# A Fourier convolution with a mixture of experts: the order of loads, gathers, scatters and gates behind the last Fourier middle

## The chip, the cores and the metric

The kernel runs on one core of one Trainium2 chip. The metric is device time in microseconds (us), the median of the runs. Engines are named as the profile names them: PE is TensorE (PEld its weight loads), DVE VectorE, ACT ScalarE, POOL GpSimd, and SP SyncE, which here only issues transfers.

## The reference, cut to what matters

```python
X = np.fft.rfft(x, axis=1)                  # x: 8 x 3072 x 256
Y = X * (filt_r + 1j * filt_i)[None]
x = np.fft.irfft(Y, n=3072, axis=1).reshape(8 * 3072, 256)
logits = x @ w_gate                         # 8 experts
expert_idx = np.argmax(logits, axis=1)
# gate_w: softmax probability of the chosen expert
# an expert keeps its first 768 tokens, in order
h = np.maximum(np.einsum('ecd,edf->ecf', disp, w1), 0.0)   # 256 -> 1024
y = np.einsum('ecf,efd->ecd', h, w2)                       # 1024 -> 256
out[i] = gate_w[i] * y[expert_idx[i], pos[i]]              # 0 for tokens not kept
```

## The kernel before, in words

The first part convolves batch after batch by a discrete Fourier transform in two steps on PE. As the experts are full after some two batches, only batches 0 and 1 and the first rows of batch 2 are transformed. `Conv.middle` multiplies by the filter, goes back by one step and leaves the result in the tiles V; `ti` transposes V on DVE, and `ai` (for the last batch `ai_last`) makes the rows and the router's logits, which SP writes to the DRAM buffer ybuf (L406). `route` finds each token's place in its expert and builds, by matmuls with one-hot tiles (L517), the table of tokens by slot; `row_of_slot` (L134) makes of it the index idxg.

The second part takes the 8 experts in order. An expert has 6 tiles of 128 tokens, in two chunks of three, (e, 0) and (e, 1). POOL gathers a chunk's rows from ybuf by three indirect DMAs (`gather`, L537). `turn` transposes them (L551, 12 matmuls) and splits them into a high half xh on ACT (L558) and a low half xl on DVE (L562). `up_steps` has 8 steps of 6 matmuls of 384 columns (L577), each followed by a split of h on ACT and DVE. `down_steps` has one step for each tile, 24 matmuls (L629); ACT scales the result by the token's gate into ob (L632) and POOL scatters it to the output (L633). `gate` makes the softmax gate of a chunk in six small DVE operations and an Exp on ACT (L596); for the chunks (0, 0) and (1, 0) it is `early_gate`, which starts at L849.

`load_part` brings a weight: a plain load of the 1024 KB to the tile raw (L660), four or two cuts on ACT that leave the rounded half wah or wbh and the negative of it in wal or wbl, and then a DMA on POOL's queue that adds the weight to that from DRAM (L673, `accum_op=ALU.add`), 512 KB each. `zero` writes 2 MB of zeros to the output (L142); `zero_late` does so beside the loads of later experts.

What sets the order is the program text: under `tc.manual_schedule()` every engine runs its instructions as they are written, and each engine's queue is first in, first out. Chunk (0, 0) and chunk (1, 0) are gathered early, while the last batch is still being made. PSUM has seven banks in rotation. The stretch between the last middle and `steady`, as it stands before:

```python
R[e, 1] = load_rows(e, 1)        # for e = 0, 1
up((1, 0), (), 1)
prep((0, 1))                     # turn and gate
up((0, 1), (), 0)
load_a, cut_a = load_part(2, "a", raw, w0)
load_a()
R[2, 0] = load_rows(2, 0)
down((1, 0), idxs0)
prep((1, 1))
up((1, 1), list(cut_a), 1)
R[2, 1] = load_rows(2, 1)
down((0, 1))
```

Of the kernel before, what the change touches and what calls it, by code (L numbers as in the profile page):

```python
# [13 lines left out]
ALU = mybir.AluOpType  # L14
# [74 lines left out]
def fftconv_moe_kernel(ctx, tc, x, fr, fi, fny, wg, w1, w2, ca, cai, cb, co, out, cap):  # L89
    nc = tc.nc  # L90
# [4 lines left out]
    NTOK = NB * SEQ  # L95
    NB0 = min(NB, -(-E * cap // SEQ) + 1)
    NF = FF // 128
    NE = min(3, NT)
    EE = 2
# [22 lines left out]
    idxs = glob.tile([128, NSLOT], I32, name="idxs")  # L122
    idx0 = glob.tile([128, EE * NT], I32, name="idx0")
    idxs0 = glob.tile([128, EE * NT], I32, name="idxs0")
# [23 lines left out]
    def zero_late(n):  # L148

        for _ in range(min(n, len(zlate))):  # L150
            apart(zero(zlate.pop(0)), "scatter", "rows behind the tokens that are routed ahead of the branch")

    def apart(ins, group, reason):
        tc.declare_no_dep(ins.ins, group=group, reason=reason)
        tc.add_to_no_dep_group(group, ins.ins)
# [7 lines left out]
    def run(fs):  # L163
        for f in fs:
            f()
# [366 lines left out]
    W, X, Gt, H = {}, {}, {}, {}  # L532
# [31 lines left out]
    def new_H(ci, n=3):  # L564
        h = hps[ci].tile([128, 2, NF, chunks[0][1] * 128], F32R, name="h", tag="h")[:, :, :, :n * 128]
        return [h[:, 0], h[:, 1]]

    def up_steps(e, x, hs, t0, n):
        o = slice(t0 * 128, (t0 + n) * 128)

        def step(m):
            (xh, xl), (ah, al) = x, W[e][:2]
            ps = bank()
            k = 0
            for kk in range(2):
                for w, y in ((ah, xh), (ah, xl), (al, xh)):
                    nc.tensor.matmul(ps[:, :n * 128], w[:, kk, m * 128:(m + 1) * 128], y[:, kk, o], start=k == 0, stop=k == 5)  # L577
                    k += 1
            split(hs[0][:, m, :], hs[1][:, m, :], ps[:, :n * 128], True)
        return [lambda m=m: step(m) for m in range(NF)]  # L580

    R, sm = {}, {"group": "scatter"}
# [3 lines left out]
    def load_rows(e, ci):  # L586
        t0, n = chunks[ci]
        rows = sm["rows"].tile([128, n, CH], F32, name="rows", tag="rows", bufs=sm["nrows"])
        gather(rows, idxg, e * NT + t0, n, (NB0 - 1) * SEQ + LAST * N2)
        return rows  # L590
# [12 lines left out]
    def prep(k):  # L603
        rows, n = R.pop(k), chunks[k[1]][1]
        X[k] = turn(rows, n, sm["p"])
        lg = sm["p"].tile([128, n, E], F32, name="lg", tag="lg")
        nc.vector.tensor_tensor(out=lg, in0=rows[:, :, 128:136], in1=rows[:, :, 136:144], op=ALU.add)
        gate(lg, n, k)

    def up(k, fill=(), place=None):  # L610
        n = chunks[k[1]][1]
        H[k] = new_H(k[1] if place is None else place)
        for m, f in enumerate(up_steps(k[0], X.pop(k), H[k], 0, n)):
            f()
            if fill and m % 2:
                fill.pop(0)()

    def down_steps(k, ix=None):
        e, (t0, n) = k[0], chunks[k[1]]
        hh, hl = H.pop(k)  # L620
        bh, bl = W[e][2], W[e][3]
        gt = Gt.pop(k)

        def step(i):
            ps = bank()
            o = slice(i * 128, (i + 1) * 128)
            for m in range(NF):
                for j, (y, w) in enumerate(((hh, bh), (hh, bl), (hl, bh))):
                    nc.tensor.matmul(ps[:, :D], y[:, m, o], w[:, m, :], start=m == 0 and j == 0, stop=m == NF - 1 and j == 2)  # L629
            ob = sm["p"].tile([128, D], F32, name="ob", tag="ob", bufs=4)  # L630
            j = e * NT + t0 + i
            nc.scalar.activation(out=ob, in_=ps[:, :D], func=AF.Copy, scale=gt[:, i:i + 1])  # L632
            ins = nc.gpsimd.indirect_dma_start(out=out, out_offset=bass.IndirectOffsetOnAxis(ap=(idxs if ix is None else ix)[:, j:j + 1], axis=0),  # L633
                                               in_=ob, in_offset=None, bounds_check=NTOK - 1, oob_is_err=False)
            apart(ins, sm["group"], "the slots' tokens differ")
        return [lambda i=i: step(i) for i in range(n)]

    def down(k, ix=None):
# [8 lines left out]
        nc.vector.tensor_tensor(out=te, in0=te, in1=tf, op=ALU.add)  # L647
        nc.vector.tensor_copy(ix, te)

    def load_part(e, part, raw, pool, parts=2, dma=None, add=True):  # L650

        src = w1[e].rearrange("(k p) f -> p k f", p=128) if part == "a" else w2[e].rearrange("(k p) d -> p k d", p=128)
        shape = [128, src.shape[1], src.shape[2]]
        h, l = (pool.tile(shape, F32R, name="w" + part + c, tag="w" + part + c, bufs=1) for c in "hl")
        W.setdefault(e, [None] * 4)[slice(0, 2) if part == "a" else slice(2, 4)] = [h, l]
        box = []

        def load():
            box.append(raw.tile(shape, F32, name="raw", tag="raw"))
            (dma or nc.sync).dma_start(out=box[0], in_=src)  # L660

        def cut(k):
            w = shape[1] * shape[2] // parts
            r, fh, fl = (t.rearrange("p n f -> p (n f)")[:, k * w:(k + 1) * w] for t in (box[0], h, l))
            nc.scalar.copy(fh, r)
            if not add:
                nc.gpsimd.tensor_tensor(out=fl, in0=r, in1=fh.bitcast(F32), op=ALU.subtract)
                return
            nc.scalar.activation(out=fl, in_=r, func=AF.Copy, scale=-1.0)
            if (k + 1) * 2 % parts == 0:  # L670
                n = shape[1] // 2
                o = slice((k * 2 // parts) * n, (k * 2 // parts + 1) * n)
                nc.gpsimd.dma_start(out=l[:, o, :], in_=src[:, o, :], accum_op=ALU.add)  # L673
        return load, [lambda k=k: cut(k) for k in range(parts)]

    def load_w(e, raw, pool):
        cuts = []
        for part in "ab":
            load, cut = load_part(e, part, raw, pool)
            load()  # L680
            zero_late(1)
            cuts += cut
        return cuts

# [80 lines left out]
    with tc.manual_schedule():  # L765
# [44 lines left out]
        for b in range(NB0 - 1):  # L810
# [5 lines left out]
            counts, sums, slots, masks, table = route(L, False, (ohp, ohp))  # L816
# [7 lines left out]
            if b + 2 == NB0:  # L824
                side_ctx.close()
                w0 = run_ctx.enter_context(tc.tile_pool(name="w0", bufs=1, side="right"))
                raw0 = run_ctx.enter_context(tc.tile_pool(name="raw0", bufs=1, side="right"))
# [9 lines left out]
        b = NB0 - 1  # L837
# [9 lines left out]
        def early_gate(e):  # L847
            lg = ep.tile([128, NE, E], F32, name="lg", tag="lg", bufs=2)
            nc.vector.tensor_tensor(out=lg, in0=early_x[e][:, :, 128:136], in1=early_x[e][:, :, 136:144], op=ALU.add)  # L849
            gate(lg, NE, (e, 0))  # L850
# [4 lines left out]
        def early_row(e, t):  # L855
# [2 lines left out]
        fill[0].append(cut_a[0])  # L858
        fill[1] += [early_index, cut_a[1]]
        fill += [[cut_a[2], lambda: early_row(0, 0)], [cut_a[3], load_b, lambda: early_row(0, 1)], [lambda: early_row(0, 2)], [last_fill],  # L860
                 [cut_b[0]], [cut_b[1]], [cut_b[2]], [cut_b[3]]]
        cv.middle(V, fill, ahead, last=[early_turn])
        top_ctx.close()
        w1p = run_ctx.enter_context(tc.tile_pool(name="w1p", bufs=1, side="right"))
        hps = [run_ctx.enter_context(tc.tile_pool(name="hp0", bufs=1, side="right"))]
        ep1 = run_ctx.enter_context(tc.tile_pool(name="ep1", bufs=1, side="right"))
        es = top_ctx.enter_context(tc.tile_pool(name="es", bufs=1))
        load_a, cut_a = load_part(1, "a", raw0, w1p, 4, add=False)
        load_b, cut_b = load_part(1, "b", raw0, w1p, 4, nc.gpsimd)
        load_a()  # L870
        L = new_L(True)
        counts, sums, slots, masks, table = route(L, True, (ohp, ohp))
# [11 lines left out]
        ti(V, 3, 4)  # L884
        run([early[4], cut_a[0], early[5], cut_a[1], early[6], cut_a[2], early[7], cut_a[3]])
        load_b()
        early_gate(0)
        for q in range(2, 4):
            ti(V, q)
        run(first)  # L890
        sm["p"] = es
        later = down_steps((0, 0), ix=idxs0)
        later[0]()
        run(counts)
        run(rest[:1])
        sums()
        run(cut_b[:2])
        run(rest[1:])
        run(slots)
        run(cut_b[2:3])  # L900
        later[1]()
        run(cut_b[3:])
        run(masks)
        X[1, 0] = turn(early_x[1], NE, ep1)
# [11 lines left out]
        smp = run_ctx.enter_context(tc.tile_pool(name="sm", bufs=2))  # L916
        raw = run_ctx.enter_context(tc.tile_pool(name="raw", bufs=2))
        sm.update(p=smp, rows=smp, nrows=3)
        for e in range(EE):
            R[e, 1] = load_rows(e, 1)  # L920
        scatter_rows(idxs, NSLOT)
        up((1, 0), (), 1)
        prep((0, 1))
        up((0, 1), (), 0)
        load_a, cut_a = load_part(2, "a", raw, w0)
        load_a()
        R[2, 0] = load_rows(2, 0)
        down((1, 0), idxs0)
        prep((1, 1))
        up((1, 1), list(cut_a), 1)  # L930
        R[2, 1] = load_rows(2, 1)
        down((0, 1))
        load_b, cut_b = load_part(2, "b", raw, w0)
        load_b()
        for ci in range(NC):
            prep((2, ci))
        later = down_steps((1, 1))
# [107 lines left out]
```

## Time and profile before

| | |
|---|---|
| time, median of 3 runs | 506.05 us (505.30 to 507.09) |
| profiled execution: time, span | 507.01 us, 505.30 us |
| PE busy | 482.8 us (96%) |
| ACT, DVE, POOL busy | 268.6, 238.6, 198.8 us |
| mean granted PE clock | 0.984 of full speed |
| moved by DMA | 96.01 MB |

The span runs from the first to the last instruction; the time of the same execution is 1.71 us longer. Times in the text are us from the span's start. The Fourier part ends in the last middle (about 160 to 193 us). Behind it the rows of the last batch and the first chunks of experts 0 and 1 are mixed (193 to 222), then come the remaining chunks of these two experts (222 to 291), and from 291 us on `steady` for experts 2 to 7. In a row of the timeline or of the waits, "<-" in brackets names the instruction that ended an engine's idle time; it is put down to the one that came last by the profile.

### The profile page before, as it was taken

To read this page: it belongs to the slowest core of one execution; us is meant where nothing else is said; L and a number is where in the kernel's file an instruction comes from. 1 tells how busy PE (TensorE), PEld (TensorE's weight loads), DVE (VectorE), ACT (ScalarE), POOL (GpSimd) and SP (SyncE) were. 2 spreads that over 40 slices of the span, in tenths; PEclk is the share of its full clock that TensorE was granted. 3 is DMA by queue.
4 is the path that set the end of the run, shared out by engine and by line. 5 is a ranking of instruction groups with operands and counts; after the bars stand their busy time and mean duration, and the time that the engine had idled before them with its cause. 6 is when DMAs were issued, how large, how long until landed. Compare 5 with 4: busy or idle time off the path is not lost.

```text
span 505.3 us, 10342 instructions
## 1 busy us (share of the span) xinstructions
PE 482.8 (96%) x4060; PEld 472.9 (94%) x4060; DVE 238.6 (47%) x529; ACT 268.6 (53%) x622; POOL 198.8 (39%) x238
## 2 busy tenths in 40 slices
PE   8999999999999999894999899999999999999995
PEld 6989999999999999893989899999999999999994
DVE  0297746776656888863322342342253243423510
ACT  3535767356666787362344557276284392473421
POOL 2165120452103874437025365175174364553022
PEclk9999999999999999997899899999999999999999
DMA  8997180990817655698008599989989989383001
GB/s 232 321 347 299 42 218 10 240 344 1 220 48 216 149 106 146 177 209 247 12 32 200 210 272 323 298 320 231 312 272 266 340 266 227 121 150 93 12 23 47
DMA packets 60570, 96.01 MB, mean 190 GB/s; under 512 B 4320, under 2 KB 37472, under 8 KB 60384
## 3 DMA queue, kind: packets, MB, share of 16 engines
q1 hardware_dynamic: 45168, 65.50, 40.5%
q0 software_dynamic: 15344, 29.76, 27.0%
q8 instruction: 34, 0.56, 0.5%
q14 instruction: 24, 0.20, 0.1%
HBM read 54.87 MB, written 40.37 MB: 188 GB/s over the span
## 4 chain that ended last, share of the span: by engine, by line
PE 64%; issue 16%; POOL 9%; DVE 4%; DMA 4%; ACT 2%; POOLq 1%; SPq 0%; DVEq 0%
PE ps L577 17%; PE ps L629 15%; PE ps L248 9%; PE ps L374 6%; PE ps L305 5%; PE ps L272 4%; PE ps L319 4%; POOL y L633 3%; DMA rows<-ybuf,idxg 3%; POOL rows L537 2%; POOL wal L673 1%; PE ps L551 1%; ACT Q L264 1%; POOL t L292 1%; DVE V L363 1%
## 5 line engine op out<-in xcount | busy, mean ns | idle before, releaser
L629 PE MATMUL ps<-wbh,h 128*128 128x256 f32 x768 | 142.2, 285 | 0.0
L629 PEld LDWEIGHTS ps<-wbh,h 128*128 128x128 f32 x768 | 121.1, 192 | 0.8 <-DVE gt L600 0.2
L560 DVE SCALAR_TENSOR_TENSOR h<-ps,h 128x384 fp32r<-128x384 f32 x128 | 67.2, 554 | 104.0 <-ACT h L558 104.0
L629 PE MATMUL ps<-wbl,h 128*128 128x256 f32 x384 | 108.9, 284 | 0.0
L633 POOL DMA_INDIRECT y<-ob,idxs x48 | 48.5, 1011 | 118.5 <-ACT ob L632 111.5
L577 PE MATMUL ps<-xh,wah 128*128 128x384 f32 x256 | 87.4, 341 | 1.9 <-ACT xh L558 1.9
L577 PE MATMUL ps<-xl,wah 128*128 128x384 f32 x256 | 87.3, 341 | 0.4 <-DVE xl L562 0.2
L577 PE MATMUL ps<-xh,wal 128*128 128x384 f32 x256 | 86.9, 339 | 0.0
L558 ACT ACTIVATE h<-ps 128x384 fp32r<-128x384 f32 x128 | 59.3, 497 | 38.4 <-PE ps L577 37.2
L629 PEld LDWEIGHTS ps<-wbl,h 128*128 128x128 f32 x384 | 73.6, 192 | 0.0
L632 ACT ACTIVATE ob<-ps,gt 128x256 f32<-128x256 f32 x48 | 22.7, 477 | 85.1 <-PE ps L629 47.3
L577 PEld LDWEIGHTS ps<-xh,wah 128*128 128x128 f32 x256 | 48.9, 191 | 2.4 <-ACT xh L558 2.2
L577 PEld LDWEIGHTS ps<-xl,wah 128*128 128x128 f32 x256 | 48.8, 191 | 1.3 <-DVE xl L562 1.3
L537 POOL DMA_INDIRECT rows<-ybuf,idxg x42 | 42.9, 1022 | 17.0 <-issue 11.0
L292 POOL TENSOR_TENSOR t<-t,t 128x256 f32<-128x256 f32 x33 | 25.0, 756 | 61.0 <-DVE t L288 56.6
L577 PEld LDWEIGHTS ps<-xh,wal 128*128 128x128 f32 x256 | 48.8, 191 | 0.0
L562 DVE TENSOR_TENSOR xl<-ps,xh 128x384 fp32r<-128x384 f32 x32 | 16.2, 548 | 61.1 <-ACT xh L558 61.1
L308 ACT CAST yh<-ps 128x408 fp32r<-128x408 f32 x48 | 24.0, 499 | 32.9 <-PE ps L305 31.5
L305 PE MATMUL ps<-IG,t 128*128 128x136 f32 x288 | 38.5, 281 | 1.9 <-POOL t L293 1.9
L248 PEld LDWEIGHTS ps<-A,xt 96*128 96x128 f32 x320 | 36.4, 192 | 1.9 <-issue 1.7
L305 PEld LDWEIGHTS ps<-IG,t 128*128 128x128 f32 x288 | 35.4, 190 | 2.9 <-POOL t L293 2.9
L248 PE MATMUL ps<-A,xt 96*128 96x128 f32 x320 | 37.2, 276 | 0.8 <-DMA xt<-x 0.8
(127 smaller groups left out, 757.7 us busy)
## 6 DMA issues: line engine op xcount, KB each, us to landing
y<-zt SPq DMA_DIRECT2D x12, 2048.0 KB, 21.8
raw<-w SPq DMA_DIRECT2D x15, 1024.0 KB, 11.8
wbl<-w POOLq DMA_DIRECT2D x16, 512.0 KB, 13.4
xt<-x SPq DMA_DIRECT2D x20, 384.0 KB, 5.9
wal<-w POOLq DMA_DIRECT2D x14, 512.0 KB, 7.6
ybuf<-rt SPq DMA_DIRECT2D x20, 162.0 KB, 2.5
ybuf<-rt SPq DMA_DIRECT2D x16, 192.0 KB, 3.3
V<-x SPq DMA_DIRECT2D x4, 384.0 KB, 7.9
```

Source lines behind the costliest of these rows:

```text
L248: nc.tensor.matmul(ps[:, i * w:(i + 1) * w], xt[:, i, h * 128:(h + 1) * 128], A[:, i * QP:i * QP + w], start=True, stop=True)
L292: eng.tensor_tensor(out=t1[:, :, 0, :], in0=t1[:, :, 0, :], in1=t2[:, :, 1, :], op=ALU.subtract)
L305: nc.tensor.matmul(ps[:, i * 136:(i + 1) * 136], self.ysb[(p // 4, h)][:, (p % 4) * 128:(p % 4 + 1) * 128], self.IG[:, h, :], start=True, ...
L308: nc.scalar.copy(fh[:, o], ps[:, :408])
L374: nc.tensor.matmul(ps[:N1, i * w:(i + 1) * w], AI[:, n0 + i, :], V[h][:, :, n0 + i, :], start=True, stop=True)
L537: nc.gpsimd.indirect_dma_start(out=rows[:, t, :], out_offset=None, in_=yrows[:lim, :], in_offset=bass.IndirectOffsetOnAxis(ap=idx[:, j + t ...
L558: nc.scalar.activation(out=hi, in_=ps, func=AF.Relu if relu else AF.Copy)
L560: nc.vector.scalar_tensor_tensor(out=lo, in0=ps, scalar=0.0, in1=hi.bitcast(F32), op0=ALU.max, op1=ALU.subtract)
L577: nc.tensor.matmul(ps[:, :n * 128], w[:, kk, m * 128:(m + 1) * 128], y[:, kk, o], start=k == 0, stop=k == 5)
L629: nc.tensor.matmul(ps[:, :D], y[:, m, o], w[:, m, :], start=m == 0 and j == 0, stop=m == NF - 1 and j == 2)
L632: nc.scalar.activation(out=ob, in_=ps[:, :D], func=AF.Copy, scale=gt[:, i:i + 1])
L633: ins = nc.gpsimd.indirect_dma_start(out=out, out_offset=bass.IndirectOffsetOnAxis(ap=(idxs if ix is None else ix)[:, j:j + 1], axis=0), i ...
```

## The change

Six things change place; no computation is added or removed.

1. The two adds of wbl for expert 1 and the last scatter of chunk (0, 0) are put off (lists `adds` and `scatters`) and go on POOL's queue behind the first three gathers of chunk (0, 1).
2. `up_over` puts the turn and the gate of the next chunk ahead of the last step of an up layer.
3. Expert 2's two loads go on ACT's queue, the first behind the layer (0, 1), the second behind the down layer (0, 1); before they stood on SP's.
4. Expert 2's rows are gathered ahead of the layer (0, 1).
5. The gate of chunk (0, 0) is made in the last middle, in its last slot for filling work.
6. Zeros are written beside the loads of experts 4 to 7, not 3 to 6.

```diff
-    def down_steps(k, ix=None):
+    def down_steps(k, ix=None, scatters=None):
...
-            ins = nc.gpsimd.indirect_dma_start(out=out, out_offset=bass.IndirectOffsetOnAxis(ap=(idxs if ix is None else ix)[:, j:j + 1], axis=0),
-                                               in_=ob, in_offset=None, bounds_check=NTOK - 1, oob_is_err=False)
-            apart(ins, sm["group"], "the slots' tokens differ")
+
+            def scatter():
+                ins = nc.gpsimd.indirect_dma_start(out=out, out_offset=bass.IndirectOffsetOnAxis(ap=(idxs if ix is None else ix)[:, j:j + 1], axis=0),
+                                                   in_=ob, in_offset=None, bounds_check=NTOK - 1, oob_is_err=False)
+                apart(ins, sm["group"], "the slots' tokens differ")
+            scatter() if scatters is None else scatters.append(scatter)
...
-                nc.gpsimd.dma_start(out=l[:, o, :], in_=src[:, o, :], accum_op=ALU.add)
+                f = lambda: nc.gpsimd.dma_start(out=l[:, o, :], in_=src[:, o, :], accum_op=ALU.add)
+                f() if adds is None else adds.append(f)
...
-            zero_late(1)
+            zero_late(1 if e > EE + 1 else 0)
...
-                 [cut_b[0]], [cut_b[1]], [cut_b[2]], [cut_b[3]]]
+                 [cut_b[0]], [cut_b[1]], [cut_b[2]], [cut_b[3], lambda: early_gate(0)]]
...
+        adds, scatters = [], []
         load_a, cut_a = load_part(1, "a", raw0, w1p, 4, add=False)
-        load_b, cut_b = load_part(1, "b", raw0, w1p, 4, nc.gpsimd)
+        load_b, cut_b = load_part(1, "b", raw0, w1p, 4, nc.gpsimd, adds=adds)
...
-        early_gate(0)
...
-        later = down_steps((0, 0), ix=idxs0)
+        later = down_steps((0, 0), idxs0, scatters)
         later[0]()
         run(counts)
         run(rest[:1])
         sums()
+        run(scatters[:1])
         run(cut_b[:2])
...
         later[1]()
+        run(scatters[1:2])
         run(cut_b[3:])
...
-        for e in range(EE):
-            R[e, 1] = load_rows(e, 1)
+        R[0, 1] = load_rows(0, 1)
+        run(adds + scatters[2:])
+        R[1, 1] = load_rows(1, 1)
         scatter_rows(idxs, NSLOT)
-        up((1, 0), (), 1)
-        prep((0, 1))
-        up((0, 1), (), 0)
-        load_a, cut_a = load_part(2, "a", raw, w0)
+
+        def up_over(k, place, f):
+
+            H[k] = new_H(place)
+            steps = up_steps(k[0], X.pop(k), H[k], 0, NE)
+            run(steps[:-1])
+            f()
+            run(steps[-1:])
+
+        up_over((1, 0), 1, lambda: prep((0, 1)))
+        R[2, 0] = load_rows(2, 0)
+        R[2, 1] = load_rows(2, 1)
+        up_over((0, 1), 0, lambda: prep((1, 1)))
+        load_a, cut_a = load_part(2, "a", raw, w0, dma=nc.scalar)
         load_a()
-        R[2, 0] = load_rows(2, 0)
         down((1, 0), idxs0)
-        prep((1, 1))
         up((1, 1), list(cut_a), 1)
-        R[2, 1] = load_rows(2, 1)
         down((0, 1))
-        load_b, cut_b = load_part(2, "b", raw, w0)
+        load_b, cut_b = load_part(2, "b", raw, w0, dma=nc.scalar)
         load_b()
```

On POOL, between the logits of the last batch (L403) and the gathers of the second chunks; y<-ob is a scatter, wbl<-w an add, rows<-ybuf a gather. Lines of the changed file are a few higher:

```order
 L403 TENSOR_TENSOR L<-rt_2776 128x32
-L633 DMA y<-ob,idxs_73 24576x256
-L673 DMA wbl<-w 128x4x256
-L633 DMA y<-ob,idxs_73 24576x256
-L673 DMA wbl<-w 128x4x256
-L633 DMA y<-ob,idxs_73 24576x256
+L635 DMA y<-ob,idxs_73 24576x256 x2
+L537 DMA rows<-ybuf,idxg 128x272 x3
+L676 DMA wbl<-w 128x4x256 x2
+L635 DMA y<-ob,idxs_73 24576x256
 L537 DMA rows<-ybuf,idxg 128x272 x9
```

Three gathers pass both adds and one scatter; nine more, expert 2's second three now among them, follow.

On ACT, from the layer (1, 0) to the first cut of expert 2's weights, first before:

```order
L558 ACTIVATE h<-ps 128x384 x8
L558 ACTIVATE xh<-ps 128x6x64 x2
L596 ACTIVATE lg<-lg 128x24
L558 ACTIVATE h<-ps 128x384 x8
L632 ACTIVATE ob<-ps,gt 128x256 x3
L558 ACTIVATE xh<-ps 128x6x64 x2
L596 ACTIVATE lg<-lg 128x24
L558 ACTIVATE h<-ps 128x384 x2
L665 CAST wah<-raw 128x1024
```

and of the change:

```order
L558 ACTIVATE h<-ps 128x384 x7
L558 ACTIVATE xh<-ps 128x6x64 x2
L596 ACTIVATE lg<-lg 128x24
L558 ACTIVATE h<-ps 128x384 x8
L558 ACTIVATE xh<-ps 128x6x64 x2
L596 ACTIVATE lg<-lg 128x24
L558 ACTIVATE h<-ps 128x384
L663 DMA raw<-w 128x2x1024
L632 ACTIVATE ob<-ps,gt 128x256 x3
L558 ACTIVATE h<-ps 128x384 x2
L668 CAST wah<-raw 128x1024
```

Both turns stand one step earlier in their layers (the eight between them are one step of the first layer and seven of the second), and the load of expert 2's first weight stands on ACT ahead of the down layer.

## Rows read from the trace of the kernel before

**Rows 1.** Windows: us, busy us (instructions) by engine, PEclk, DMA share, GB/s.
```profile
241.00:243.00 2.00, 2.00 (x8) 2.00 (x8) 0.56 (x1) 0.49 (x1) 0.00 (x0) 0.50 0.00 0
281.00:283.00 2.00, 2.00 (x13) 2.00 (x12) 1.47 (x5) 0.71 (x3) 0.00 (x0) 0.59 1.05 410
300.00:400.00 100.00, 100.00 (x767) 99.40 (x766) 32.58 (x89) 52.21 (x98) 43.19 (x42) 1.00 1.02 294
```

**Rows 2.** Who PE waits for, 205 to 291 us: total us, times, longest us.
```profile
PE ps L551 <- issue: 5.4, 1, 5.4
PE ps L577 <- ACT xh L558: 1.9, 2, 1.0
PE ps L398 <- DVE V L363: 1.4, 1, 1.4
PE ps L551 <- DVE xl L562: 1.1, 1, 1.1
PE ps L551 <- DMA rows<-ybuf,idxg: 0.5, 2, 0.3
PE ps L577 <- DVE xl L562: 0.2, 1, 0.2
```

**Rows 3.** Chain that ended last, 222 to 317 us: start, us, what.
```profile
222.24 4.38 PE ps L577 x24
...
238.60 11.18 PE ps L577 x48
...
280.71 10.23 PE ps L629 x72
290.94 16.64 PE ps L577 x96
307.58 8.62 PE ps L629 x72
316.20 0.89 PE ps L551 x24
```

**Rows 4.** Timeline of POOL, 219 to 232 us: start, us, instruction, idle before.
```profile
220.36 1.38 POOL L673 DMA_DIRECT2D wbl<-w  x1
...
227.74 1.06 POOL L537 DMA_INDIRECT rows<-ybuf,idxg  x1 [4.48 <-DVE h L560]
...
230.43 1.01 POOL L537 DMA_INDIRECT rows<-ybuf,idxg  x1 [0.30 <-issue]
```

**Rows 5.** DMA issues near 215, 218, 221, 197, 231, 265, 205, 312: us to landing.
```profile
ybuf<-rt SPq DMA_DIRECT2D x2, 256.0 KB, 3.5
...
ybuf<-rt SPq DMA_DIRECT2D x2, 256.0 KB, 8.0
...
wbl<-w POOLq DMA_DIRECT2D x1, 512.0 KB, 14.6
...
rows<-ybuf,idx POOLq DMA_INDIRECT x1, 2.9
...
rows<-ybuf,idxg POOLq DMA_INDIRECT x1, 6.5
...
wal<-w POOLq DMA_DIRECT2D x1, 512.0 KB, 5.7
...
raw<-w POOLq DMA_DIRECT2D x1, 1024.0 KB, 6.7
...
raw<-w SPq DMA_DIRECT2D x1, 1024.0 KB, 20.6
```

**Rows 6.** Timeline of DVE (202 to 211 us) and of ACT (213 to 221).
```profile
202.84 0.81 DVE L849 TENSOR_TENSOR lg<-rows 128x24 f32<-128x24 f32 x1
...
205.70 4.48 DVE L363 STREAM_TRANSPOSE V<-V 128x2048 f32<-128x2048 f32 x2
...
213.49 1.08 ACT L400 COPY rt<-ps 128x512 f32<-128x512 f32 x2 [4.01 <-DMA ybuf<-rt]
...
219.93 0.89 ACT L558 ACTIVATE xh<-ps 128x384 fp32r<-128x384 f32 x2
```

More of the change, by code (lines that the diff above doesn't have):

```diff
@@ L648, in scatter_rows, with load_part @@
         nc.vector.tensor_copy(ix, te)
-    def load_part(e, part, raw, pool, parts=2, dma=None, add=True):
+    def load_part(e, part, raw, pool, parts=2, dma=None, add=True, adds=None):
         src = w1[e].rearrange("(k p) f -> p k f", p=128) if part == "a" else w2[e].rearrange("(k p) d -> p k d", p=128)
```

## The prediction

> **What bounds the kernel now.** I read three views in this order: who PE waits for in the stretch behind the last middle, the chain that ended last, and the windows with the granted clock. PE is the bound: from 300 to 400 us it is busy for all of its 100.00 us at clock 1.00 [rows 1], and it waits for nothing from 291 us to the end. So the last 214 us are matmuls alone, and time can only be won ahead of them. PE's waits between 205 and 291 us [rows 2] are six: 1.4 us for DVE's transposes of V, 5.4 us ahead of a turn (named "issue"; the rows that it transposes were in flight), 1.9 us in two places for the xh halves of a turn, 1.1, 0.5 and 0.2 us. The second loss is the clock: behind the 5.4 us wait the granted clock falls to 0.50, which is 1.2 GHz, and behind the waits near 280 us to a mean of 0.59 [rows 1]. In the chain [rows 3] the first expert layer behind the wait, 48 matmuls, takes 11.18 us; 96 of the same kind take 16.64 us later, so 8.32 for 48. A down layer of 72 matmuls takes 10.23 us at 280.71 and 8.62 us at 307.58.
>
> The account of the stretch: expert 1's first layer starts at 222.24 and expert 2's at 290.94 [rows 3], 68.7 us. The work in it is three up layers (3 x 8.32 = 24.96), three down layers (3 x 8.62 = 25.86) and four turns (two pairs at 0.89), in all 52.6 us. So **16.1 us of it are lost**: 9.1 us of waits [rows 2] (the 1.4 lies ahead of the stretch), 2.86 + 1.61 us in two layers at the slow clock, and some 2.5 us in turns that were slowed or spread out.
>
> **Why the rows are late.** POOL issues expert 0's second gathers from 227.74 us on, after 4.48 us of waiting [rows 4]. The program makes that gather wait for the last writes of ybuf; DVE, which the row names, is only the last to be seen. Those writes land 8.0 us after issue, while a pair 3 us earlier took 3.5 [rows 5]: between the two came the first adding load of wbl, then expert 2's loads. The third gather is issued at 230.43 [rows 4] and takes 6.5 us [rows 5], behind a second adding load (220.36) that needs 14.6 us. With no such neighbour a gather took 2.9 us [rows 5].
>
> **The change part by part.**
>
> *Adds and the third scatter behind the first three gathers, expert 2's loads later.* Nothing is added; two adding loads, one scatter and two 1024 KB loads change place. The writes of ybuf then have only a scatter beside them, and I give them 3.5 us: issued at about 218.3, landed by 222. The index that the gathers need is written at about 222 too, behind the xl of the turn (its xh is ACT's at 219.93 to 220.8 [rows 6]). So the gathers go from about 222.5 instead of 227.74, the third at 225.2, and it lands at 228 with 2.9 us, or at 231.7 with the 6.5 of now. PE asks for them after seven of eight steps of expert 1's layer, 7 x 1.04 us behind its start at 221.8 (below), at 229.1. I take 0.3 us of waiting; the ends are 0 and 2.6.
>
> *Behind them on POOL's queue.* The adds go at 226.4 and 227.8, the scatter at 229, then expert 1's second gathers at about 230.5 to 234. Adds cost 5.7 us alone and 14.6 in the crowd of now [rows 5]; the crowd (2 MB of loads) is gone, so two of them should land by 236 and the gathers by 237.5. PE wants these rows after seven steps of the next layer, at 238.5: cover of 1 us. The adds themselves are first read by the down layer at 240.1, cover of 4 us. I cost this at nothing; if the cover goes, it is the first rival.
>
> *Turns ahead of a layer's last step.* No instruction more. Now PE stands about 0.95 us for xh and another 0.2 for xl behind each turn [rows 2]. With six matmuls (1.04 us) in between, the wait for xh is gone; the second matmul of the next layer still comes too early for xl, by about 0.35 us at the first place (0.95 + 0.2 + one matmul's 0.17, less 1.04, rounded up for ACT's order). At the second place a whole down layer of 8.6 us lies in between: nothing. On ACT and DVE the last step's h stands behind the turn's gate; it is read only a layer later.
>
> *Expert 2's loads on ScalarE's queue, its rows earlier.* The first load goes out behind the second layer, at about 240, and is cut after 10.6 us (a down layer and two steps); alone such a load takes 6.7 us [rows 5]. The second goes out at about 266 and is cut some 3.5 us later, so ACT waits about 3 us there. PE doesn't: with seven banks it can run past ACT by two down groups (5.7 us) and five steps (5.2 us). Expert 2's rows are gathered by 245 and wanted at 265, so the waits of 1.1 + 0.5 us near 280 and the slow 1.61 us behind them go.
>
> *No writes of zeros with expert 3's loads.* The same eight writes come with experts 4 to 7 instead of 3 to 6. PE waited nowhere beside them [rows 1], and expert 7's stage gets what expert 6's had: nothing.
>
> *Gates in the middle.* DVE spends 202.84 to 205.70 on the gate, then 4.48 us on two transposes of V [rows 6]; PE's 1.4 us wait is behind these. Moved away, the wait goes, but ACT's work until the next turn doesn't start earlier: at 213.49 it waits 4.01 us for writes of ybuf, and then runs without a pause to the xh at 219.93 [rows 6]. Expert 1's layer could start at 221.5 at best, 0.7 us earlier. In the middle the gate holds up DVE and ACT in front of the last casts of yh: at least nothing, at most its 2.86 us; I take 0.3, near the lower end, since PE has finished yh tiles to go on with there. Net gain 0.4; ends -2.2 and +1.4.
>
> **Sum.** 16.1 lost, of which 0.35 (xl), 0.3 (first rows) and 0.25 (draining of two single turns) stay: 15.2 won, and 0.4 for the gate: 15.6. The profiled execution has a span of 505.30 and a time of 507.01, 0.96 above the median of its runs; 505.3 - 15.6 = 489.7 for the span, and the median 506.05 goes to **490.5**.
>
> **Rivals.**
>
> *Expert 1's rows come late behind the adds.* For it: the adds stand ahead of these gathers in POOL's own queue, and one add took 14.6 us [rows 5]. Then the second add lands at 227.8 + 14.6 = 242.4, the rows a us later; PE stands 4.9 us at the second turn and the clock falls as it did, 2.86 + 0.95 us. That leaves 6.9 of the gain: 499.2. Against: that add shared the engines with 2 MB that are gone. The Trainium skill, DMA: Bandwidth & Descriptors, section "Two DMAs through the same engine are not ordered", says that descriptors of one queue on one engine start in order; by that rule alone the move of the adds only hands the delay from the first rows to the next ones, and the time would be this rival's 499. The trace agrees on the order: nothing that POOL queued behind the second add landed ahead of its 235.0.
>
> *The first gathers start no earlier.* If the writes of ybuf are slow by themselves, the first gather stays at 227.3, the third lands at about 234, PE stands 5 us and falls to the slow clock: gain 7, time 499. Against: 3.5 us for the pair 3 us before.
>
> *Slower: ACT stands behind a late load.* ACT's cuts wait for expert 2's loads, and every eviction is behind them. Afterwards they are asked for only 10.6 and 3.5 us ahead. Loads took 6.7 to 20.6 us [rows 5]. At 20.6 each, and 2 us of cutting behind them, ACT is held until 263 (240 + 22.6) and, with the delay so far, until 296 (273 + 22.6); PE runs out of banks at 260 and at 287: 3.4 + 8.7 us, 2 more to catch up, and the slow clock twice (3.8 each): 21.7 us, 6.1 more than the 15.6 won, time 512. Even is at about 18 us for both; below 11.7 us nothing is lost. The load of 20.6 had writes of zeros around it, which now begin one expert later. The Trainium skill, TensorE: Matmul & The Clock Gate, "Engine queue depths", calls ScalarE's queue strictly first in, first out: by it nothing behind the cut could pass. No row here shows an eviction passing one.
>
> *No effect*: the wait comes back elsewhere in full, 505.5.
>
> **How the numbers follow.** Forecast 0.70 (488.5 to 493), late second rows 0.12, gathers no earlier 0.08, no effect 0.05, ACT held 0.05. The low end is 16.1 with all of the 1.4 us: 488.5. The forecast's own range holds it nine times in ten (0.63); the two cases at 499, which cost less if the delay is partial, must come in, so the high end is 499.2, and 0.8 is inside. A measurement of this kernel can tell 0.3%, 1.5 us: all cases down to 499 are faster, 0.91 with part of "no effect"; same 0.04, slower 0.05.
>
> **What would show it.** First gather on POOL at about 222.5; no PE wait over 1 us from 205 to 275; clock 1.00 throughout; expert 2's first layer at about 275 instead of 290.94, and from there 214 us as now. Wrong if PE waits at either turn for rows, if ACT idles before a cut for over 8 us, or if the last 214 us grow.

## The result, and the profile after

The changed kernel takes **493.7 us** (median of 4 runs, 493.0 to 493.95); the kernel before had 506.57 beside it. The ratio is 0.9748, with a 95% interval of 0.9716 to 0.978: faster by 12.9 us, where 15.6 were forecast. The forecast of 490.5 was 3.2 too low, and its own range for the likeliest case (488.5 to 493) was left by 0.7; the range of all cases holds it. The profiled execution took 493.74 us with a span of 492.0.

Windows of after (us, busy us by engine, PEclk, DMA share, GB/s), the same three as in [rows 1]:

```profile
241.00:243.00 2.00, 2.00 (x18) 2.00 (x17) 1.61 (x7) 0.71 (x3) 1.70 (x2) 1.00 0.42 107
281.00:283.00 2.00, 2.00 (x13) 2.00 (x12) 1.11 (x2) 0.90 (x3) 1.62 (x2) 1.00 1.01 290
300.00:400.00 100.00, 100.00 (x754) 99.19 (x753) 35.00 (x95) 53.41 (x104) 47.11 (x47) 1.00 1.00 286
```

The granted clock is 1.00 at the times where it was 0.50 and 0.59 (by then the program is a stage further on), and its mean from 205 to 291 us is 1.00. Who PE waits for in after, 205 to 291 us:

```profile
PE ps L551 <- DMA rows<-ybuf,idxg: 0.2, 1, 0.2
PE ps L577 <- DVE xl L562: 0.2, 1, 0.2
```

Of the six groups of [rows 2] two are left, 0.2 us each. The chain of after, beside [rows 3]:

```profile
222.30 2.33 PE ps L577 x12
...
227.46 2.81 DMA rows<-ybuf,idxg
...
241.56 8.51 PE ps L629 x72
250.08 8.32 PE ps L577 x48
258.40 8.62 PE ps L629 x72
267.91 8.71 PE ps L629 x72
276.62 16.64 PE ps L577 x96
```

From 241.56 us on every layer has its full speed, 8.32 for 48 matmuls and 8.5 to 8.7 for 72. From expert 1's first layer to expert 2's it is 276.62 - 222.30 = 54.3 us, where it was 68.7: 14.4 of the 15.2 forecast. POOL in after, beside [rows 4]:

```profile
220.19 1.00 POOL L635 DMA_INDIRECT y<-ob,idxs  x1 [7.89 <-ACT ob L632]
224.80 1.04 POOL L537 DMA_INDIRECT rows<-ybuf,idxg  x1 [3.61 <-PE ps L577]
...
227.46 1.00 POOL L537 DMA_INDIRECT rows<-ybuf,idxg  x1 [0.30 <-issue]
228.45 2.84 POOL L676 DMA_DIRECT2D wbl<-w  x2
231.60 1.08 POOL L635 DMA_INDIRECT y<-ob,idxs  x1 [0.30 <-ACT xh L558]
232.99 1.10 POOL L537 DMA_INDIRECT rows<-ybuf,idxg  x1 [0.30 <-issue]
```

The first gather goes at 224.80; forecast was 222.5. In DMA issues of after, near 219.5, 224.5, 232.8 and 404 us:

```profile
ybuf<-rt SPq DMA_DIRECT2D x1, 256.0 KB, 4.5
...
rows<-ybuf,idxg POOLq DMA_INDIRECT x3, 2.9
...
rows<-ybuf,idxg POOLq DMA_INDIRECT x3, 4.2
...
y<-ob,idxs POOLq DMA_INDIRECT x1, 17.3
```

The last write of ybuf takes 4.5 us (8.0 in [rows 5]), the first gathers 2.9, and those behind the adds 4.2.

The rest of the account lies outside this middle stretch, which is 14.4 us shorter. The stretch from the turn of chunk (0, 0) to expert 1's first layer went from 31.0 to 29.6 us (the gate, 1.4 won). That turn itself came 1.4 us later, at 192.6 for 191.2 us; in the other profiled runs it comes at 191.4 to 193.4. The gate now stands ahead of this turn (188.8 to 190.5 us), but it isn't the cause: in all fourteen profiles the last 100 matmuls ahead of the turn take 12.9 us and the last 1600 take 167.5 to 167.6, with the gate among them or not, so the 1.4 us arise in the first 25 us of the run. And from expert 2's first layer to the end it is 215.4 us and no longer 214.4. Together 14.4 + 1.4 - 1.4 - 1.0 = 13.4, where the spans give 505.3 - 492.0 = 13.3. The 1.0 is read from three rows of after: who waits, 276 to 492 us, for ACT and for PE, and PE at 421 us.

```profile
ACT ob L632 <- DMA y<-ob,idxs: 32.7, 4, 9.2
...
PE ps L577 <- ACT ob L632: 0.5, 1, 0.5
...
421.94 0.44 PE L577 MATMUL ps<-xh,wah 128*128 128x384 f32 x1 [0.48 <-ACT ob L632]
```

ACT has four tiles ob; for the fifth tile of an expert it waits until the scatter of the first has landed. Before, this wait was 8.5 us at most and PE felt nothing; now it is 9.2 behind the scatter of 17.3 us, and PE stands 0.5 us. The two up layers of that expert take 17.39 us in a row, those of the expert before it 16.82, where 16.64 is the rule: 0.9 of the 1.0 us lie in these two pairs.

### The profile page after: what moved, and what is told of

It reads as the page before. It is cut to its first block, busy times and chain, and to the rows that moved or that the text cites. A ratio compares the mean times of both kernels' runs of the same rounds, so it can differ in the third digit from the quotient of the medians.

```text
span 492.0 us, 10336 instructions
## 1 busy us (share of the span) xinstructions
PE 478.8 (97%) x4060; PEld 470.3 (96%) x4060; DVE 236.1 (48%) x529; ACT 268.1 (54%) x622; POOL 199.0 (40%) x238
## 4 chain that ended last, share of the span: by engine, by line
PE 70%; issue 11%; POOL 6%; DMA 5%; DVE 3%; ACT 2%; POOLq 0%; SPq 0%; DVEq 0%; ACTq 0%
PE ps L577 19%; PE ps L629 18%; PE ps L248 9%; PE ps L374 6%; PE ps L305 5%; PE ps L272 5%; PE ps L319 4%; DMA y<-ob,idxs 4%; POOL y L635 2%; PE ps L398 2%; POOL rows L537 1%; DVE t L288 1%; PE ps L551 1%; ACT Q L264 1%; POOL wal L676 1%
## 5 line engine op out<-in xcount | busy, mean ns | idle before, releaser
L629 PE MATMUL ps<-wbh,h 128*128 128x256 f32 x768 | 140.7, 283 | 0.0
L629 PEld LDWEIGHTS ps<-wbh,h 128*128 128x128 f32 x768 | 119.9, 190 | 0.8 <-issue 0.4
L577 PE MATMUL ps<-xl,wah 128*128 128x384 f32 x256 | 86.2, 337 | 0.4 <-DVE xl L562 0.4
L248 PEld LDWEIGHTS ps<-A,xt 96*128 96x128 f32 x320 | 38.5, 202 | 1.8 <-issue 1.8
L248 PE MATMUL ps<-A,xt 96*128 96x128 f32 x320 | 38.9, 286 | 1.1 <-DMA xt<-x 1.1
```

The source lines that it names most:

```text
L248: nc.tensor.matmul(ps[:, i * w:(i + 1) * w], xt[:, i, h * 128:(h + 1) * 128], A[:, i * QP:i * QP + w], start=True, stop=True)
```

## The experiments

All ratios are against the kernel before, run on the same chip. "Middle" is from expert 1's first layer to expert 2's, "last" from there to the end, both of the profiled run, by the first matmul of each layer (0.1 to 0.2 us ahead of the pieces of the chain). A pair of up layers is the two up layers of one expert, 96 matmuls in a row; "theory" and "rival" are those of the expectation above each result. Each profile is one execution.

| kernel | ratio (95%) | middle, us | last, us |
|---|---|---|---|
| before | 1 | 68.6 | 214.5 |
| the change | 0.9748 (0.9716 to 0.978) | 54.2 | 215.6 |
| u_adds: change, adds and scatters at once | 0.9876 (0.9803 to 0.9948) | 62.7 | 215.8 |
| u_loads: change, expert 2's loads on SP | 0.9777 (0.9739 to 0.9815) | 57.7 | 216.4 |
| u_turn: change, turns behind the layer | 0.9753 (0.9706 to 0.9799) | 54.8 | 215.6 |
| u_gate: change, gate behind the middle | 0.9786 (0.9748 to 0.9824) | 53.8 | 215.8 |
| u_zero: change, zeros with experts 3 to 6 | 0.9879 (0.985 to 0.9908) | 55.4 | 221.8 |
| o_adds: before, adds and scatter put off | 0.9881 (0.985 to 0.9913) | 60.4 | 216.1 |
| o_loads: before, expert 2's loads on ACT | 1.0047 (1.002 to 1.0074) | 63.6 | 220.3 |
| p_loads: o_loads, zeros with experts 4 to 7 | 0.9946 (0.9924 to 0.9968) | 62.7 | 215.7 |
| x_spread: change, zeros spread otherwise | 0.9782 (0.9749 to 0.9815) | 54.6 | 218.5 |
| x_ob: change, six tiles ob | 0.9718 (0.969 to 0.9746) | 53.8 | 214.4 |
| z_ob: u_zero, six tiles ob | 0.9764 (0.9733 to 0.9794) | 53.9 | 216.2 |
| b_ob: before, six tiles ob | 0.9949 (0.9929 to 0.9968) | 67.2 | 214.5 |

### One part undone at a time

**u_adds.**

```diff
-        load_b, cut_b = load_part(1, "b", raw0, w1p, 4, nc.gpsimd, adds=adds)
+        load_b, cut_b = load_part(1, "b", raw0, w1p, 4, nc.gpsimd)
-        later = down_steps((0, 0), idxs0, scatters)
+        later = down_steps((0, 0), idxs0)
```

> The change with one part undone: the two adds of expert 1's second weight and the three scatters go out as soon as they are ready, ahead of the first gathers. My theory: the crowd was made by adds and expert 2's loads together, and with the loads gone the adds alone cost little: the last writes of ybuf land in about 5 us instead of 4.5, the second add (issued near 221) lands near 229, and the third gathered row set comes 1 to 2 us later than in the change; about 2 us slower than the change (496). Rival: the place of the adds is the main cause; then the first turn waits 5 us again and the clock falls, 8 us slower (502).

Measured: 500.69 us. The rival was nearer. Waits of PE in the profile of u_adds, its POOL, and the DMA issues near 217 us:

```profile
PE ps L551 <- issue: 5.1, 1, 5.1
```

```profile
216.88 1.39 POOL L676 DMA_DIRECT2D wbl<-w  x1 [5.78 <-ACT wbl L672]
...
230.83 1.06 POOL L537 DMA_INDIRECT rows<-ybuf,idxg  x1 [7.80 <-DVE h L560]
```

```profile
wbl<-w POOLq DMA_DIRECT2D x1, 512.0 KB, 7.6
ybuf<-rt SPq DMA_DIRECT2D x2, 256.0 KB, 9.2
```

With expert 2's loads issued only behind the next layer, the adds and scatters by themselves hold the last two writes of ybuf to 9.2 us (the median of the two), and the wait ahead of the turn is back. Their place is the main part of the middle: 8.5 of the 14.4 us. The last scatter moved together with the two adds; no run moves one without the other, so that it is the adds (1024 KB against one scatter of 128 rows) is likely, not shown.

**u_loads.** `dma=nc.scalar` is left out of both `load_part(2, ...)`.

> The change with one part undone: expert 2's two loads stand on SP's queue again, where they are issued as soon as the writes of ybuf are out, near 221. My theory: 2 MB beside the first gathers make the gathers land in 6 us instead of 2.8 and the second set late behind the adds; PE waits 3 to 5 us at a turn and its clock falls: 6 to 9 us slower than the change (500 to 503). Rival: where the loads stand doesn't matter once the gathers are ahead of the adds; within 1 us of the change.

Measured: 495.65 us. Both expectations missed: the loads are worth 3.5 us in the middle of the profiled run, which was the slowest of its four (497.73); by the ratios it is some 1.5 us, and the two intervals overlap. The first gather still goes at 225.09, but the rows land 5.5 us after issue (median), for 2.9 in the change, and PE waits:

```profile
PE ps L551 <- DVE h L560: 1.4, 1, 1.4
PE ps L551 <- DMA rows<-ybuf,idxg: 0.7, 1, 0.7
```

**u_turn.**

```diff
-            run(steps[:-1])
-            f()
-            run(steps[-1:])
+            run(steps)
+            f()
```

> The change with one part undone: turns and gates stand behind a layer's last step again. Theory: each of the two turns shows its wait for xh and xl again (0.95 + 0.2 us) less the 0.2 that is left now, and the first loses its short wait for rows: 1.5 us slower than the change (495.2). Rival: nothing, since the rows bound the first turn anyway and the second's wait moves into a down layer: under 0.5 us.

Measured: 494.67 us, and 0.6 us more in the middle; the ratios can't tell the two kernels apart. One wait for xh is back among PE's waits:

```profile
PE ps L577 <- ACT xh L558: 1.0, 1, 1.0
```

The other isn't: here too a down layer, which needs none of its rows, stands behind the second turn. The turn's place inside the layer is worth about 0.6 us.

**u_gate.** `early_gate(0)` goes back behind `load_b()`.

> The change with one part undone: the gate of chunk (0, 0) stands ahead of the last transposes of V again. Theory from the profile of the change: it is worth 1.3 us, because its Exp on ACT also held back the first copies of the last rows and so the writes of ybuf; 1.3 us slower (495.0). Rival, the prediction's step: ACT's chain hides most of it, 0.4 us slower (494.1).

Measured: 495.65 us. The wait for V is back among PE's waits:

```profile
PE ps L398 <- DVE V L363: 1.4, 1, 1.4
```

From the turn of chunk (0, 0) to expert 1's first layer it is 31.0 us as before, not 29.6: this stretch is 29.6 to 29.7 us in the eight profiles with the gate in the last middle and 31.0 in the six without. The gate's place is worth the 1.4 us of its wait.

### The zeros, and parts of the change alone

**u_zero.** `zero_late(1)` for every expert again.

> The change with the zeros written beside the loads of experts 3 to 6 again. Theory: with the change the stretch from expert 2's first layer to the end is 215.4 us, where it was 214.4, because expert 7's zeros hold up a scatter (17.3 us), this holds ACT's ob, and PE waits 0.5 us and drains slowly; so here the stretch falls back to about 214.4 and the time to 492.7, with no wait for ob. Rival: the 1.0 us is chance and turns up beside another expert's zeros: 215.4, time 493.7. Second rival: expert 3's zeros lie beside expert 2's second load and the adds, ACT or PE waits there for over 1 us, and the time is 495 or more.

Measured: ratio 0.9879, some 6.6 us above the change, the largest miss of the study: both the theory and the first rival said that nothing would be lost; the second rival had the place and not the price. Five views of u_zero follow it: ACT at 277 us, POOL from 282 us, two pieces of the chain, ACT from 308 us, and PE's waits from 291 to 345 us; the last line is POOL's in z_ob (below).

```profile
277.24 1.05 ACT L668 CAST wbh<-raw 128x1024 fp32r<-128x1024 f32 x1 [3.93 <-DMA raw<-w]
```

```profile
282.26 1.44 POOL L676 DMA_DIRECT2D wbl<-w  x1
...
296.18 1.97 POOL L676 DMA_DIRECT2D wal<-w  x2 [3.13 <-ACT h L558]
297.37 3.40 POOL L676 DMA_DIRECT2D wbl<-w  x2
301.08 1.09 POOL L635 DMA_INDIRECT y<-ob,idxs  x1 [0.30 <-issue]
```

```profile
282.26 13.24 DMA wbl<-w
...
301.08 19.83 DMA y<-ob,idxs
```

```profile
308.34 0.46 ACT L632 ACTIVATE ob<-ps,gt 128x256 f32<-128x256 f32 x1
321.02 0.91 ACT L632 ACTIVATE ob<-ps,gt 128x256 f32<-128x256 f32 x2 [12.22 <-DMA y<-ob,idxs]
```

```profile
PE ps L577 <- ACT ob L632: 3.7, 1, 3.7
```

```profile
295.15 1.96 POOL L676 DMA_DIRECT2D wal<-w  x2 [4.03 <-DMA wbl<-w]
```

Zeros that SP sends out at 258.43 are beside expert 2's second load, which ACT now waits 3.9 us for. The adds of wbl that follow come late; the second, at 282.26, 0.3 us behind more zeros, takes 13.2 us (its piece in the chain). Expert 3's four adds, which go out 2.7 us apart in the change, are held until that one has landed (z_ob, which has the same bunch, names it as what POOL waited for) and then leave within 4.6 us, straight ahead of the scatters of expert 2. The first of these takes 19.8 us, ACT stands 12.2 for its tile and PE 3.7, PE's mean granted clock from 320 to 340 us is 0.91 for 1.00 in the change, and expert 3's up layers take 22.2 us instead of 16.6. So part 6 isn't an extra: it makes room for part 3.

**o_adds** is before with the lists `adds` and `scatters` of the diff, and nothing else.

> The kernel before, with the two adds and the last scatter put off behind the first three gathers, and nothing else. Theory: the place of the adds stands on its own; undoing it cost 7.0 us, so doing it alone brings about 7: 499, first gather near 225 and the wait of 5.4 us ahead of the turn down to about 1. Rival: the two loads for expert 2, still issued at 221 beside the last writes of ybuf, take part of it back: 502 or more, first gather at 226 or later, and a wait of 2.5 us or more.

Measured: ratio 0.9881, 6.0 us, a little short of the theory's 7; in the middle 8.2 us are won, and 1.6 are lost again in the last stretch, where PE waits for ob (1.1 us in all). The first gather goes at 224.85, as the theory said, and the last writes of ybuf land in time, with expert 2's loads beside them (DMA issues near 218 us):

```profile
ybuf<-rt SPq DMA_DIRECT2D x2, 256.0 KB, 5.0
```

The place of the adds, with the last scatter's, stands on its own.

**o_loads** is before with `dma=nc.scalar` in both `load_part(2, ...)`.

> The kernel before, with expert 2's two loads on ScalarE's queue, and nothing else. Theory: undoing them cost 2.0 us, and the adds alone delay the writes of ybuf to 9 to 11 us, so the first gather stays at 227 or later and the time is 504 to 505. Rival: without the 2 MB of loads beside them the writes land in 3.5 us and the first gather goes at 223.5 or earlier: 499.

Measured: ratio 1.0047, slower, which neither side had expected. The first gather comes 5.6 us behind the layer's start, as before, for the writes of ybuf are as late as before, with the adds beside them and the loads gone (DMA issues near 221 us):

```profile
ybuf<-rt SPq DMA_DIRECT2D x2, 256.0 KB, 8.1
```

In the middle 5.0 us are won all the same; in the last stretch 5.8 are lost, and PE's wait from 300 to 350 us tells where:

```profile
PE ps L577 <- ACT ob L632: 2.7, 1, 2.7
```

It is u_zero's case again: expert 3's up layers take 22.4 us. **p_loads** takes the zeros away from there, by the diff's line in `load_w`.

> The kernel before, with expert 2's loads on ScalarE's queue and the zeros moved to experts 4 to 7: parts 3 and 6 together. Theory: part 3 alone made expert 3's up layers take 22.4 us, since expert 2's adds then lay beside expert 3's loads and zeros; with the zeros gone there they take 16.64, the ratio falls from 1.0047 by 0.0114 (5.8 of 506 us) to 0.993, and part 6 is a part of part 3. Rival: expert 3's loads alone crowd the adds, the layers still take 19 us or more, and the ratio is 1.0 or more.

Measured: 0.9946, as the theory said. Expert 3's up layers take 16.64 us and the last stretch 215.7.

**x_spread** leaves out zeros beside expert 3's first load and expert 7's second.

> The change with the eight zeros spread otherwise: one beside expert 3's second load, two each beside those of experts 4 to 6, one beside expert 7's first load. Theory: the 1.0 us lies in the zeros that go out behind expert 7's second load; without them the stretch from expert 2's first layer to the end is 214.4 us and the time 492.7, as with the zeros on experts 3 to 6. Rival: chance, 493.7. Second rival: expert 3's zeros cost what expert 7's did, 493.7 with an ACT or PE wait near 277 to 300 us.

Measured: 0.9782. The theory fell, and both rivals with it: four pairs of up layers, of experts 3 to 6, take 17.5 to 17.8 us each, and the last stretch is 218.5. Moving one block of zeros moves the waits for ob about; it doesn't remove them. Why the four stages came out equally bad stays open.

### Six tiles ob

```diff
-            ob = sm["p"].tile([128, D], F32, name="ob", tag="ob", bufs=4)
+            ob = sm["p"].tile([128, D], F32, name="ob", tag="ob", bufs=sm.get("obs", 4))
...
-        sm.update(p=smp, rows=smp, nrows=3)
+        sm.update(p=smp, rows=smp, nrows=3, obs=6)
```

**x_ob** is the change with this.

> The change with six tiles ob in the steady part instead of four, so that ACT need not wait for a scatter of the same expert. Theory: the late layers lose time (16.82 and 17.39 us for a pair of up layers instead of 16.64) only because ACT stands 7 to 9 us in each stage for a scatter that lands 15 to 17 us after issue; with six tiles ACT's wait for ob behind a scatter is gone (32.7 us in the change), each pair of up layers takes 16.64, and the time is 492.7, 1.0 below the change. Rival: the scatters land late all the same and hold up POOL's queue, so that the wait moves to the rows or the adds of the next expert, and the time is that of the change, 493.7, or more.

Measured: 492.13 us, ratio 0.9718. ACT's waits from 260 us on, and the only waits of PE from 190 us on:

```profile
ACT ob L632 <- PE ps L629: 50.9, 24, 2.4
ACT h L558 <- PE ps L577: 35.8, 66, 0.6
```

```profile
PE ps L577 <- DVE xl L562: 0.4, 2, 0.2
```

ACT waits for no scatter, every pair of up layers takes 16.64 us, the last stretch is 214.4: as the theory said. It is the fastest of the kernels here; its interval and the change's overlap, so that it beats the change is read from the stretch (1.1 us, one profile each), not from the ratios alone.

**z_ob** has u_zero's zeros as well.

> The change with the zeros beside the loads of experts 3 to 6 again, and six tiles ob in the steady part. Theory: the zeros beside expert 3's loads cost through ob alone: a scatter of expert 2 took 19.8 us beside them, ACT stood 12.2 us for ob, and the up layers behind took 22.2 us instead of 16.64. With six tiles they take 16.64 again and the time falls from 0.9879 of the kernel before to 0.976 or less. Rival: the crowd delays what else stands there too (adds of 13 us, expert 3's weights and rows), PE still waits 2 us or more near 300 to 345 us, and the ratio stays at 0.982 or more.

Measured: 0.9764, by a hair over the theory's 0.976. Of the 7.3 us that u_zero lost in the last stretch against x_ob 5.5 come back, expert 3's up layers take 16.64 us, and of what is left (1.8 us) the most is another wait:

```profile
PE ps L629 <- DMA wbl<-w: 1.3, 1, 1.3
```

The adds themselves come late for expert 2's second down layer. So the crowd costs in two ways, and ob was the larger.

**b_ob** is before with six tiles.

> The kernel before, with six tiles ob in the steady part and nothing else. Theory: before the change ACT waited up to 8.5 us for a scatter in a stage, but PE waited for nothing behind 291 us; the four tiles bind only where a later schedule uses up that slack, so here they bring nothing: ratio 1.000, each pair of up layers 16.64 us as before, last stretch 214.4. Rival: the tiles are a gain of their own, that has nothing to do with the change: 0.997 or less.

Measured: 0.9949, outside what the theory allowed. The rival's number is met, but the two profiles show no difference in the last stretch (214.5 and 214.5). They differ in the middle, 67.2 for 68.6 us; whether by the tiles or by chance no run shows. Of eleven profiles with four tiles, that of before is the only one in which PE doesn't wait for ob. It is likely that other runs of before do wait; that is argued, since no trace of one was taken.

## Why the prediction was right, and where it was off

The main mechanism came true: the first rows are there in time, no wait over 0.2 us is left from 205 to 291 us, and the clock stays at 1.00. Two steps failed, that of the gate and that of the zeros, and one term, the draining of the turns, was too small.

*The late rows.* Right: adds beside the writes of ybuf were the cause. Which of the two neighbours counts was left open there, and u_adds, o_adds, u_loads and o_loads part them: 8.5 and 8.2 us for the adds with the scatter, 3.5 and 5.0 for the loads. The last write of ybuf takes 8.0 to 11.2 us with the adds and the scatter beside it (before, u_adds, o_loads, p_loads) and 4.2 to 5.2 without, and it makes no clear difference there whether expert 2's loads are near (5.0 in o_adds and u_loads). In all profiles that show its landing the first gather goes 1.1 to 1.5 us behind it. The loads act later, on the rows themselves: 5.5 us beside them in u_loads, 2.9 in the change.

*First gather at 222.5.* Off by 2.3 us, at no cost. The last write of ybuf was issued at 219.1 and not at 218.3 (the whole opening was 1.4 us late), took 4.5 us where 3.5 was taken, and the gather went 1.1 us behind it; the index was there at 223.0. With the gate gone ACT could have made the last copies earlier, but it waits ahead of them for expert 1's second weight:

```profile
215.34 0.62 ACT L668 CAST wbh<-raw 128x512 fp32r<-128x512 f32 x1 [2.33 <-DMA raw<-w]
```

The turn asked for the rows at 230.1, where 229.1 was forecast, and waited 0.23 us; 0.3 was taken.

*Second rows behind the adds.* Right to put the loss at nothing: they landed 5.3, 4.2 and 3.3 us after issue. The rival of 499 did not come, and with it the forecast by the Trainium skill's rule (DMA: Bandwidth & Descriptors, "Two DMAs through the same engine are not ordered"): the descriptors may start in order here too, but two adds without 2 MB beside them held the rows behind them for 2.4 us at most (5.3 for 2.9), and PE waited for none of these rows.

*Turns.* The wait for xl was 0.19, with 0.35 forecast ([rows 2] has the 0.2 us for xl once, and not behind each turn as the prediction read it); the place inside the layer is worth 0.6 us, because the order of turn and down layer hides the second wait by itself, as u_turn shows. Mis-sized: 0.25 for the draining of two single turns. The two up layers with a turn in each take 19.3 us (222.30 to 241.56), where two layers and two single turns make 17.5; 0.4 of the 1.7 us are waits, the other 1.3 lie around the turns. With this the middle lost 1.7 us and not 0.9, and that is the 0.8 that it fell short.

*Expert 2's loads on ACT.* They landed in 5.3 and 5.8 us, and ACT waited 0.4 us instead of 3. That holds only with the zeros gone: in u_zero and z_ob ACT waited 3.9 and 4.2 us for the second load.

*Expert 2's rows earlier.* Right, though no run undoes this part alone: the two turns ahead of expert 2 take 0.9 us in the nine profiles with it, u_loads among them, and 2.0 to 3.2 in the five without (3.2 before).

*Gate.* Mis-sized: 0.4 was taken, as 0.7 won less 0.3 lost in the middle; the runs show 1.4 and nothing. The step "ACT's work until the next turn doesn't start earlier" failed: ACT's wait of 4.0 us [rows 6] had the gate's delay in it, because the gate's Exp stood ahead of the copies that feed ybuf. With the gate away the xl of the next turn, which the prediction took as the floor, ends 0.5 us sooner behind the turn of chunk (0, 0).

*Zeros: "nothing".* This step failed, and by the most. Undone, it costs 7.4 us in the profile (1.2 in the middle, 6.2 in the last stretch). The prediction judged parts 3 and 6 apart, where o_loads, p_loads and u_zero show that part 3 without 6 loses what it wins. That the sum held is luck on this point: the two were made together.

*"PE waits for nothing from 291 us to the end."* True of that one trace, and too weak a ground. ACT's wait for a scatter in before, 260 to 500 us:

```profile
ACT ob L632 <- DMA y<-ob,idxs: 28.9, 4, 8.5
```

Its longest was 8.5 us, and the rows of four kernels tell what it may be. ACT's wait and PE's are 9.2 and 0.5 us in the change, 9.5 and 0.9 in x_spread, 11.4 and 2.7 in o_loads, 12.2 and 3.7 in u_zero: PE waits for what is over some 8.5 to 8.7 us, an estimate from these four. Before stood close to that edge, 0.2 us at most. Of the signs of being wrong that the prediction named, one came: the last 214 us grew, by 1.0.

*The rival on the other side* named ACT held by a late DMA, banks running out, and the slow clock. That is what o_loads and u_zero show, only that ACT is held by a scatter and not by a load: before with that part alone is slower, at 1.0047.

The sum came out 15.6 - 0.8 (middle) + 1.0 (gate) - 1.0 (last) - 1.4 (opening) = 13.4, where the spans give 13.3. The misses partly cancel: the 1.0 that the gate gave more made up for the 1.0 of the last stretch, and the opening's 1.4 lies within the spread of the fourteen profiles, whose turns start at 191.2 to 193.4 us.

## What to carry to other kernels

Adding DMAs of half a megabyte that nothing needs soon should be queued behind the small transfers that something needs now: the place of two of them, with one scatter, was worth 8 of 14 us here. When a load is moved later, look at what is issued a stage behind it, and move that too, or the loss comes back there. And where an engine shows no wait, read how long its supplier waits: 8.5 us of idle time on ACT was harmless and 9.2 were not, and two more small tiles took the wait away.

## What was not expected of the hardware

While the adds were in flight the DMA engines were busy all the time and moved little. Windows of u_adds:

```profile
220.00:228.00 8.00, 8.00 (x59) 7.58 (x58) 6.01 (x22) 3.81 (x10) 2.73 (x3) 1.00 1.09 191
234.00:240.00 6.00, 4.33 (x21) 3.83 (x22) 1.94 (x9) 1.48 (x4) 4.55 (x5) 0.50 0.39 111
```

A DMA share of 1.09 goes with 191 GB/s, where in [rows 1] a window at a share of 1.05, in which zeros were written, had 410. The packets of the first window are smaller too, nearly all under 2 KB (1880 of 1923), and none are in the other; how much of the difference is the adding and how much the size is not shown. The second row is the price behind it: six us at a granted clock of 0.50, that is 1.2 GHz, after PE had stood 5.1 us. And a scatter of 128 rows, which lands in 3.8 us at 220 us, took 17.3 and 19.8 us beside adds, a load and zeros.
